# Retention of 128-position chunks recomputed in steps of 64 positions with 64x64 products, and a seven-product down projection with chained sums

## The chip, the core and the metric

The kernel runs on one core of a Trainium2 chip. Its parts, as the profile names them: PE (TensorE, matrix products; PEld is its loading of the stationary operand, which overlaps the products), DVE (VectorE), ACT (ScalarE), POOL (GpSimd), SP (SyncE, which here issues DMA). Products write to PSUM, which DVE and ACT empty. The metric is the device time of one execution in microseconds (us), and lower is better.

## What is computed

Batch 8, 8 heads, 576 positions, head size 64. For each head `h` the retention is causal and decays with distance; after it, 4608 tokens of width 512 go through an up product to 2048, an activation, and a down product to 512.

```python
scores = scale * np.matmul(q, k.transpose(0, 1, 3, 2))
Dmat = np.where(rel >= 0, gamma[:, None, None] ** rel[None, :, :], 0.0)
attn = np.matmul(scores * Dmat[None], v)          # then (B*S, H*D) = x
h = x @ w_in
g = h * np.clip(h + 3.0, 0.0, 6.0) / 6.0
out = g @ w_out
```

Retention need not form all 576x576 scores. With keys scaled by `gamma**(-position)` and queries by `gamma**position` inside a chunk, a chunk's output is a masked product inside the chunk (scores, then scores times values) plus the query times a 64x64 state per head that sums keys times values of all earlier positions.

## The kernel before

**Blocks.** The first 64 positions of all eight batches form block 0, handled by functions whose names end in `heads`. The other 512 positions of each batch are blocks 1 to 8, each of four chunks of 128 positions; chunk `c` belongs to block `c // 4`, and chunks 4 to 35 pass through the functions below. The output of a block's retention is the tile `xT`, which the up product of the same block reads.

**Up and down.** `up_unit` is a sixteenth of a block's up product: eight products of 512 columns into one PSUM bank `ph` (L163), then on ACT a Relu into `u` (L389), then on DVE the activation into `g` (L391). The bank is free again when L391 is done. The down product of blocks 0 and 1 is plain (`down_plain`, tile `pd`). From block 2 on, `down_strassen` uses seven half-size products instead of eight (112 steps, each a pair of matmuls of 256 columns, tile `pm`). It needs sums of quarters of `g` (five a half block, DVE, L407), sums of weight quarters made once (five pairs, `ws`, DVE), and sums of the results (ACT copies, adds on POOL and DVE).

**Retention of a chunk.** `casts` (k on ACT, q and v on POOL, with the decay), `transposes` (on PE for chunks before 13, by DMA on SP after), `scores` (L210: eight matmuls, two 64-row halves of the array at a time, 128 columns; two banks `pa`; two masked copies on DVE, L213), `state` (L245: eight matmuls of 64 columns into `pu`, an add on DVE L250, a product with the decay on POOL L251), `past` (the state to fp16 in a block-diagonal tile `sbd`, two ACT casts L237), `inner` (L264 with `product` at L163: scores times values and state times query into one bank `po`, eight matmuls each, 128 columns; one ACT copy to `xT`, L268).

**Array shapes.** The profile gives a matmul's shape as rows*columns of the array that it uses. Most of this kernel uses 128*64: `product` splits an output of 128 partitions into two halves, which run side by side. `scores` uses 64*128, and `by_key` of block 0 uses 128*32.

**Order.** Instructions stand on each engine in the order in which the code issues them (`manual_schedule`). For blocks 0 to 2 the strings given to `go` set it: a letter is a step (`c` cast, `t` transpose, `s` state, `z` past, `a` scores, `i` inner, `+` a pending DVE sum, `D` down steps, `L`, `R`, `U` up units). From block 2 on, the loop at the end runs sixteen times a block: one up unit of the next block, seven down steps of this one, then the retention steps that the table `STEADY` (for block 2 `FIRST_STEADY`) holds under that number, for chunks of the block after next:

```python
for _ in range(lead):
    next(down, None)
if kb + 1 < NB:
    up_unit(kb + 1, u)
...
for _ in range(per - lead):
    next(down, None)
do((w, i if w == "+" else c + i) for w, i in table.get(u, []))
```

**PSUM.** Of eight banks, six rotate in the pool `pp` (`ph`, `pa`, `pu`, `po` and the transposes, in the order in which they are asked for), and two in `st` (down products). A tile in `pp` takes the bank of the tile that was asked for six places earlier, and its first write waits until that one has been read.

The functions with the profile's line numbers:

Of the kernel before, what the change touches and what calls it, by code (L numbers as in the profile page):

```python
# [12 lines left out]
FP32 = mybir.dt.float32  # L13
# [8 lines left out]
def kernel(  # L22
# [54 lines left out]
    mask = const.tile([P, P], FP16)  # L77
    query = const.tile([P, P], FP32)
# [8 lines left out]
    sbd = [const.tile([P, NP, 2, D], FP16, name=f"sbd{i}") for i in range(2)]  # L87
# [46 lines left out]
    def others():  # L134
# [4 lines left out]
        for h in range(H):  # L139
            lo = (h % 2) * D  # L140
            nc.gpsimd.memset(gpow[lo:lo + D, h // 2:h // 2 + 1], float(gamma[h] ** P))
        for i in range(2):
            nc.gpsimd.memset(sbd[i], 0.0)

    def mask_of_chunk():
        nc.gpsimd.memset(mask, 1.0)
        nc.gpsimd.affine_select(out=mask, in_=mask, compare_op=ALU.is_ge,
                                fill=0.0, base=0, pattern=[[1, P]], channel_multiplier=-1)

# [5 lines left out]
    ws = {n: const.tile([P, JH, HM], FP16, name=f"ws{n}") for n in (1, 3, 4, 6, 7)}  # L155

    hmask = ws[4].rearrange("p j n -> p (j n)")[:, 0:H * P].rearrange("p (h q) -> p h q", h=H)
# [20 lines left out]
    def casts(c):  # L178
        fk, fq, fv = st[c]["f"]
        dd = dec[:, NJ, :].unsqueeze(2).to_broadcast([P, 2 * H, D])  # L180
        k16 = work.tile([P, H, D], FP16, tag="k16", bufs=4, name=f"k16_{c}")
        q16 = work.tile([P, H, D], FP16, tag="q16", name=f"q16_{c}")
        v16 = work.tile([P, H, D], FP16, tag="v16", bufs=NV16, name=f"v16_{c}")
        nc.scalar.copy(k16, fk)  # L184
        nc.gpsimd.tensor_tensor(q16, fq, dd[:, 0:H, :], ALU.mult)  # L185
# [3 lines left out]
    def transposes(c, on_pe):  # L189
        for nm in ("k", "q"):  # L190
            src = st[c][nm + "16"].rearrange("p h d -> p (h d)")
            dst = work.tile([P, NP, P], FP16, tag=f"{nm}T", bufs=4, name=f"{nm}T_{c}")
# [10 lines left out]
    def scores(c):  # L203
        kT, qT = st[c]["kT"], st[c]["qT"]
        a16 = work.tile([P, 2, NP, P], FP16, tag="a16", name=f"a16_{c}")
        pa = [psum.tile([P, NP, P], FP32, tag="pp", name=f"pa{h2}_{c}") for h2 in range(2)]
        for i in range(NP):
            for h2 in range(2):
                r = slice(h2 * D, h2 * D + D)
                nc.tensor.matmul(pa[h2][:, i, :], kT[r, i, :], qT[r, i, :], start=True, stop=True)  # L210
        m = mask.unsqueeze(1).to_broadcast([P, NP, P])
        for h2 in range(2):
            nc.vector.tensor_tensor(a16[:, h2], pa[h2], m, ALU.mult)  # L213
        st[c]["a16"] = a16
# [510 lines left out]
```

## Time and profile before

| what | value |
|---|---|
| median of 3 runs | 301.76 us (300.6 to 302.05) |
| the profiled execution | 300.82 us |
| its span on the core | 299.1 us |
| mean granted clock of PE | 0.994 |
| PE busy | 289.9 us (97%), 4514 matmuls |
| DVE, ACT, POOL busy | 237.9, 199.9, 151.4 us |

The span is what the profile covers; 1.7 us of the execution lie around it. Busy time counts an engine as busy while any of its instructions is under way. Matmuls overlap each other: one of 512 columns is under way for about 380 ns, but the next pair starts about 215 ns after the one before, so the starts in the timeline say more than the busy time. Granted clock 1.00 means that PE ran at full speed.

### The profile page before, as it was taken

How to read it: one execution, taken by the hardware profiler on the slowest of the kernel's cores; microseconds unless marked ns; L12 is line 12 of the kernel's file. 1: busy time of each engine (PE TensorE's matmuls, PEld its weight loads, DVE VectorE, ACT ScalarE, POOL GpSimd, SP SyncE). 2: the span in 40 equal slices, each digit the busy share in tenths (PEclk: the TensorE clock that was granted, in tenths of full speed). 3: DMA queues.
4: the chain of work that ended last, by engine and by line, in shares of the span. 5: the costliest groups of instructions: out<-in, count | busy, mean ns of one | idle time of the engine just before them, and what ended most of it. 6: DMA issues, size and time to landing. Idle time of an engine off the chain costs nothing.

```text
span 299.1 us, 10655 instructions
## 1 busy us (share of the span) xinstructions
PE 289.9 (97%) x4514; PEld 222.6 (74%) x4514; DVE 237.9 (80%) x389; ACT 199.9 (67%) x374; POOL 151.4 (51%) x182
## 2 busy tenths in 40 slices
PE   6799999999999999999999999999999999999995
PEld 2478567887665678777878787878887888778894
DVE  4739576978966868899979897989798979777972
ACT  4668966999666597766776577657765765465430
POOL 7887087555844404891388338833893353014100
PEclk9989999999999999999999999999999999999999
DMA  7999999899999999999998999999975010300122
GB/s 159 168 197 215 187 214 207 187 212 207 208 163 156 316 170 225 180 186 182 263 160 147 211 196 151 152 213 195 160 144 178 20 18 2 142 2 2 72 107 106
DMA packets 136287, 47.74 MB, mean 160 GB/s; under 512 B 125744, under 2 KB 131376, under 8 KB 136240
## 3 DMA queue, kind: packets, MB, share of 16 engines
q1 hardware_dynamic: 131088, 41.56, 72.2%
q0 software_dynamic: 4720, 5.11, 10.3%
q8 instruction: 35, 0.57, 0.8%
q10 hardware_dynamic: 432, 0.39, 0.5%
q14 instruction: 12, 0.10, 0.1%
HBM read 36.70 MB, written 9.44 MB: 154 GB/s over the span
## 4 chain that ended last, share of the span: by engine, by line
PE 83%; DMA 7%; DVE 3%; ACT 2%; SPq 1%; POOL 1%; issue 1%; POOLq 0%; DVEq 0%
PE ph L163 39%; PE pm L163 29%; PE pd L163 6%; DMA qT<-q 3%; PE pa L210 2%; PE po L163 2%; PE po L264 2%; DMA fq<-in_q_dram 2%; DMA hq<-in_q_dram 2%; DMA hk<-in_k_dram 1%; DVE g L391 1%; DVE a L213 1%; PE pu L245 1%; POOL q L185 1%; ACT u L389 1%
## 5 line engine op out<-in xcount | busy, mean ns | idle before, releaser
L163 PE MATMUL ph<-xT,win 128*64 128x512 f16 (+1 forms) x1248 | 146.4, 365 | 0.3
L389 ACT ACTIVATE u<-ph,half 128x512 f32<-128x512 f32 (+1 forms) x156 | 99.9, 657 | 59.4 <-PE ph L163 58.0
L391 DVE SCALAR_TENSOR_TENSOR g<-u,ph 128x512 f16<-128x512 f32 (+1 forms) x156 | 98.4, 643 | 37.2 <-ACT u L389 36.5
L163 PEld LDWEIGHTS <-win 128*64 128x64 f16 x1248 | 81.0, 137 | 25.0 <-issue 0.4
L251 POOL TENSOR_TENSOR z<-t,gpow 128x256 f32<-128x256 f32 x24 | 18.5, 769 | 69.8 <-DVE t L250 65.9
L163 PEld LDWEIGHTS <-g 128*64 128x64 f16 x704 | 37.9, 110 | 14.5
L163 PE MATMUL pm<-ws,s 128*64 128x256 f16 x672 | 43.8, 273 | 0.0
L163 PEld LDWEIGHTS <-s 128*64 128x64 f16 x672 | 37.0, 110 | 7.1
L185 POOL TENSOR_TENSOR q<-fq,dec 128x512 f16<-128x512 f32 x32 | 37.4, 1170 | 8.0 <-DMA fq<-in_q_dram 5.9
L407 DVE TENSOR_TENSOR s<-g 128x1024 f16<-128x1024 f16 x42 | 41.3, 988 | 0.0
L213 DVE TENSOR_TENSOR a<-pa,mask 128x512 f16<-128x512 f32 x64 | 40.3, 682 | 0.5 <-PE pa L210 0.5
L186 POOL TENSOR_TENSOR v<-fv,dec 128x512 f16<-128x512 f32 x32 | 38.6, 1208 | 0.1
L163 PE MATMUL pd<-wout,g 128*64 128x512 f16 x256 | 33.9, 381 | 0.0
L163 PE MATMUL pm<-ws,g 128*64 128x256 f16 x448 | 30.6, 273 | 0.0
L163 PE MATMUL pm<-wout,sab 128*64 128x256 f16 x448 | 30.6, 273 | 0.0
L163 PEld LDWEIGHTS <-sab 128*64 128x64 f16 x448 | 24.7, 110 | 4.8
L268 ACT CAST xT<-po 128x512 f16<-128x512 f32 x32 | 18.7, 586 | 11.9 <-PE po L163 11.8
L407 DVE TENSOR_TENSOR sab<-g 128x1024 f16<-128x1024 f16 x28 | 23.4, 839 | 0.0
L184 ACT CAST k<-fk 128x512 f16<-128x512 f32 x32 | 19.8, 619 | 0.2
L237 ACT CAST sbd<-z 64x256 f16<-64x256 f32 x48 | 19.2, 400 | 0.4
L264 PE MATMUL po<-a,v 128*64 128x128 f16 x256 | 18.1, 219 | 0.1
L163 PE MATMUL po<-qT,sbd 128*64 128x128 f16 x256 | 17.9, 219 | 0.0
(106 smaller groups left out, 272.6 us busy)
## 6 DMA issues: line engine op xcount, KB each, us to landing
fk<-in_k_dram SPq DMA_DIRECT2D x32, 256.0 KB, 4.3
fq<-in_q_dram SPq DMA_DIRECT2D x32, 256.0 KB, 4.8
fv<-in_v_dram SPq DMA_DIRECT2D x32, 256.0 KB, 5.1
out_dram<-o SPq DMA_DIRECT2D x15, 512.0 KB, 4.8
wout<-in_moe_w_out_dram POOLq DMA_DIRECT2D x4, 512.0 KB, 16.0
win<-in_moe_w_in_dram POOLq DMA_DIRECT2D x3, 512.0 KB, 9.9
out_dram<-o SPq DMA_DIRECT2D x5, 256.0 KB, 5.4
hq<-in_q_dram SPq DMA_DIRECT2D x6, 128.0 KB, 5.0
```

What stands on the lines that cost most here:

```text
L163: nc.tensor.matmul(out[r], lhs[:, r], rhs, skip_group_check=True, **flags)
L184: nc.scalar.copy(k16, fk)
L185: nc.gpsimd.tensor_tensor(q16, fq, dd[:, 0:H, :], ALU.mult)
L186: nc.gpsimd.tensor_tensor(v16, fv, dd[:, H:2 * H, :], ALU.mult)
L213: nc.vector.tensor_tensor(a16[:, h2], pa[h2], m, ALU.mult)
L237: nc.scalar.copy(sbd[i0 % 2][r, :, h2, :], z[r])
L251: nc.gpsimd.tensor_tensor(z, t, decay, ALU.mult)
L264: nc.tensor.matmul(po[h2 * D:h2 * D + D, i, :], v16[:, 2 * i + h2, :], a16[:, h2, i, :], start=(i == 0), stop=False, skip_group_check=True)
L268: nc.scalar.copy(xts[kb][:, :, i0 * P:i0 * P + P], po)
L389: nc.scalar.activation(uu[:, 0:n], ph[:, 0:n], ACTF.Relu, bias=half, scale=1.0 / 6.0)
L391: nc.vector.scalar_tensor_tensor(out=g[:, hf, ths, jr, :], in0=by_half(uu), scalar=1.0, in1=by_half(ph), op0=ALU.min, op1=ALU.mult)
L407: nc.vector.tensor_tensor(*pend.popleft())
```

## The change

A chunk is handled as two steps of 64 positions. `scores` forms only the two 64x64 diagonal squares of each head (the scores between the second half's queries and the first half's keys are replaced by the state), `states` sums keys times values of each half apart, `add` makes two states a chunk (before the first half, and before the second), `past` turns both to fp16, and the output is cross terms (state times query) and inner terms (scores times values). Every matmul of these uses 64*64 of the array and 64 columns, and the lists are issued two and two for the upper and the lower 64 rows (`in_turn`). A chunk takes 64 matmuls instead of 32 (the last chunk of a block 56 instead of 24). The two row halves are kept from adding into one bank at the same time: the cross terms that go over to the other bank (`cross_over`) come first, then the states of the next chunks, then a drain of PE (`nc.tensor.drain()`), then the rest of the cross terms and the inner terms (`inner`).

From chunk 16 on, two chunks go through these functions together, and a visit in `STEADY` is `a` of the next pair, `x` and `i` of this pair with `s` of the next between them, in steps 5 and 13 of sixteen. Chunks 4 to 15 go one at a time (scores and states share a bank there). The masked copies take half the elements, the adds on DVE go from one a chunk to two, the block-diagonal tile is gone, and heads are stored in another order so that heads `i` and `i + 4` share a transposed tile.

The down product still takes seven products of the same sizes, in the order 1, 5, 2, 3, 6, half of 4, 7, the other half of 4, with four sums of `g` a half block (each made from the one before) and four pairs of weight sums instead of five of each.

The core of the diff; removed lines of the retention functions are left out, since they stand above:

```diff
-        for i in range(2):
-            nc.gpsimd.memset(sbd[i], 0.0)
...
+        nc.gpsimd.tensor_copy(mask[SUB:P, 0:SUB], mask[SUB:P, SUB:P])
...
-        k16 = work.tile([P, H, D], FP16, tag="k16", bufs=4, name=f"k16_{c}")
-        q16 = work.tile([P, H, D], FP16, tag="q16", name=f"q16_{c}")
+        k16 = work.tile([P, NP, 2, D], FP16, tag="k16", bufs=4, name=f"k16_{c}")
+        q16 = work.tile([P, NP, 2, D], FP16, tag="q16", name=f"q16_{c}")
-        nc.scalar.copy(k16, fk)
-        nc.gpsimd.tensor_tensor(q16, fq, dd[:, 0:H, :], ALU.mult)
+        by_head = lambda t: t.rearrange("p i a d -> p a i d")
+        in_rows = lambda t: t.rearrange("p (a i) d -> p a i d", a=2)
+        nc.scalar.copy(by_head(k16), in_rows(fk))
+        nc.gpsimd.tensor_tensor(by_head(q16), in_rows(fq), in_rows(dd[:, 0:H, :]), ALU.mult)
...
+            dst = work.tile([P, NP, P], FP16, tag=f"{nm}T", bufs=dict(k=4, q=6)[nm], name=f"{nm}T_{c}")
...
+    PAIRS = 16
+    group = lambda c: [c] if c < PAIRS else [c, c + 1]
+    rows = lambda x: slice(SUB * x, SUB * x + SUB)
+    gs = {}
+    def mm(*args, **flags):
+        return lambda: nc.tensor.matmul(*args, skip_group_check=True, **flags)
+    def in_turn(by_row):
+        for n in range(0, max(len(t) for t in by_row), 2):
+            for t in by_row:
+                for x in t[n:n + 2]:
+                    x()
+    def scores(c0):
+        g = group(c0)
+        n = len(g)
+        a16 = work.tile([P, 2, 2, NP, SUB], FP16, tag="a16", bufs=4, name=f"a16_{c0}")
+        pb = [psum.tile([P, 2, NP, SUB], FP32, tag="pp", name=f"pa{a}_{c0}") for a in range(2)]
+        pa = [b[:, 0:n] for b in pb]
+        todo = ([], [])
+        for x, c in enumerate(g):
+            kT, qT = st[c]["kT"], st[c]["qT"]
+            for i in range(NP):
+                for s in range(2):
+                    for a in range(2):
+                        todo[a].append(mm(pa[a][rows(s), x, i, :], kT[rows(a), i, rows(s)], qT[rows(a), i, rows(s)],
+                                          start=True, stop=True))
+        in_turn(todo)
+        gs[c0] = dict(a16=a16, pa=pa, pu=[b[:, n:2] for b in pb])
+        if n == 2:
+            masked(c0)
+    def masked(c0):
+        n, a16, pa = len(group(c0)), gs[c0]["a16"], gs[c0]["pa"]
+        m = mask[:, 0:SUB].unsqueeze(1).to_broadcast([P, n * NP, SUB])
+        for a in range(2):
+            nc.vector.tensor_tensor(a16[:, a, 0:n].rearrange("p x i q -> p (x i) q"),
+                                    pa[a].rearrange("p x i q -> p (x i) q"), m, ALU.mult)
     decay = gpow.unsqueeze(2).to_broadcast([P, NP, D])
...
+    def states(c0):
+        g = group(c0)
+        pu = gs[c0]["pu"]
+        if len(g) == 2:
+            pu = [psum.tile([P, 2, NP, D], FP32, tag="pp", name=f"pu{s}_{c0}") for s in range(2)]
+        todo = ([], [])
+        for x, c in enumerate(g):
+            k16, v16 = st[c]["k16"], st[c]["v16"]
+            sums[c] = [pu[s][:, x] for s in range(2)]
+            for i in range(NP):
+                for s in range(2 if c % NCB < NCB - 1 else 1):
+                    for a in range(2):
+                        todo[s].append(mm(pu[s][rows(a), x, i], k16[rows(s), i, a, :], v16[rows(s), i + NP * a, :],
+                                          start=True, stop=True))
+        in_turn(todo)
+        if len(g) == 1:
+            masked(c0)
+    def state_of(c):
+        if c not in zs:
+            zs[c] = work.tile([P, 2, NP, D], FP32, tag="z", bufs=2, name=f"z{c}")
+        return zs[c]
+    def add(c):
+        kb, i0 = divmod(c, NCB)
+        z = state_of(c)
+        nc.vector.tensor_tensor(z[:, 1], sums[c][0], z[:, 0] if i0 else zh[kb - 1], ALU.add)
+        if i0 < NCB - 1:
+            new = state_of(c + 1)[:, 0]
+            nc.vector.tensor_tensor(new, sums[c][1], z[:, 1], ALU.add)
+            nc.gpsimd.tensor_tensor(new, new, decay, ALU.mult)
     def past(c):
         kb, i0 = divmod(c, NCB)
...
+        z16 = work.tile([P, 2, NP, D], FP16, tag="z16", bufs=2, name=f"z16_{c}")
+        if i0:
+            nc.scalar.copy(z16, zs[c])
+        else:
+            nc.scalar.copy(z16[:, 0], zh[kb - 1])
+            nc.scalar.copy(z16[:, 1], zs[c][:, 1])
+        z16s[c] = z16
     xts = {}
...
+    def cross(c0, flip):
+        g = group(c0)
+        todo = ([], [])
+        if "po" not in gs[c0]:
+            gs[c0]["po"] = [psum.tile([P, len(g), NP, SUB], FP32, tag="pp", name=f"po{s}_{c0}") for s in range(2)]
+        for x, c in enumerate(g):
+            for i in range(NP):
+                for a in range(2):
+                    s, cc, b = a ^ flip, i // 2 + 2 * a, i % 2
+                    todo[a].append(mm(gs[c0]["po"][s][rows(b), x, cc, :], z16s[c][rows(a), s, i, :],
+                                      st[c]["qT"][rows(a), i, rows(s)],
+                                      start=bool(flip) and x == 0 and i < 2, stop=False))
+        return todo
+    def cross_over(c0):
+        in_turn(cross(c0, 1))
+    def inner(c0):
+        kb, i0 = divmod(c0, NCB)
+        g = group(c0)
+        n = len(g)
         if kb not in xts:
             xts[kb] = work.tile([P, NP, BLK], FP16, tag="xT", bufs=2, name=f"xT{kb}")
...
+        todo = cross(c0, 0)
+        a16, po = gs[c0]["a16"], gs[c0]["po"]
+        for x, c in enumerate(g):
+            for h in range(H):
+                for s in range(2):
+                    todo[s].append(mm(po[s][rows(h % 2), x, h // 2, :], st[c]["v16"][rows(s), h, :],
+                                      a16[rows(s), h // NP, x, h % NP, :], start=False, stop=True))
+        nc.tensor.drain()
+        in_turn(todo)
+        xt = xts[kb][:, :, i0 * P:i0 * P + n * P].rearrange("p n (x s q) -> p s x n q", x=n, s=2)
+        for s in range(2):
+            nc.scalar.copy(xt[:, s], po[s])
+        for c in g:
+            del st[c], z16s[c]
+        del gs[c0]
...
-            gt[kb, jq] += [sab, s1, s67]
+            s1, s2, s3, s4 = [gp.tile([P, JQ, HB], FP16, tag=f"s{n}", bufs=b, name=f"s{n}{kb}_{jq}")
+                              for n, b in ((1, 2), (2, 2), (3, 2), (4, 2))]
+            pend.extend([(s1, g[:, 0, 1], g[:, 1, 1], ALU.add), (s2, s1, g[:, 0, 0], ALU.subtract),
+                     (s4, g[:, 1, 0], s2, ALU.subtract), (s3, g[:, 0, 0], g[:, 0, 1], ALU.subtract)])
+            gt[kb, jq] += [s1, s2, s3, s4]
...
-        prods = {1: (A(2), W(1)), 2: (A(1, 1), B11), 3: (A(0, 0, 0), W(3)), 4: (A(0, 1, 1), W(4)),
-                 5: (A(1, 0), B22), 6: (A(3, 0), W(6)), 7: (A(3, 1), W(7))}
+        lo, hi = slice(0, HM), slice(HM, DM)
+        prods = {1: (A(0, 0, 0), half_of(0, lo)), 2: (A(0, 1, 0), half_of(1, lo)), 3: (A(4), half_of(1, hi)),
+                 4: (A(0, 1, 1), W(4)), 5: (A(1), W(1)), 6: (A(2), W(2)), 7: (A(3), W(3))}
...
-        b3, by_m3 = bank(3)
-        yield from one(3, by_m3)
-        nc.scalar.copy(s3, b3)
-        b4, by_m4 = bank(4)
-        yield from one(4, by_m4)
-        nc.scalar.copy(s4, b4)
-        side.tensor_tensor(s3, s3, s4, ALU.add)
-        yield from one(5, by_m3, True)
-        nc.scalar.copy(c12, b3)
...
+        ba, by_a = bank(1)
+        yield from one(1, by_a)
+        nc.scalar.copy(p1, ba)
+        bb, by_b = bank(5)
+        yield from one(5, by_b)
+        nc.scalar.copy(p5, bb)
...
+        yield from one(2, by_a, True)
+        nc.scalar.copy(c11, ba)
...
+        yield from one(3, by_b, True)
+        nc.scalar.copy(c12, bb)
+        bc, by_c = bank(6)
+        yield from one(6, by_c)
+        nc.scalar.copy(u2, bc)
+        add(pool, u2, u2, p1)
+        add(pool, c12, c12, u2)
+        store(kb, 0, o1)
+        bd, by_d = bank(4)
+        yield from one(4, by_d, ms=(0,))
+        yield from one(7, by_c, True)
+        add(dve, u3, bc, p1)
+        add(pool, c22, p5, u3)
+        yield from one(4, by_d, ms=(1,))
+        add(dve, c21, bd, u3)
         store(kb, 1, o2)
...
-        of = {3: (b12, b22, ALU.subtract), 4: (b21, b11, ALU.subtract), 1: (b11, b22, ALU.add),
-              6: (b11, b12, ALU.add), 7: (b21, b22, ALU.add)}
+        of = {1: (b12, b11), 2: (b22, ws[1]), 3: (b22, b12), 4: (b21, ws[2])}
-                x, y, op = of[n]
-                pend.append((ws[n][:, j, :], x[:, j, :], y[:, j, :], op))
+                x, y = of[n]
+                pend.append((ws[n][:, j, :], x[:, j, :], y[:, j, :], ALU.subtract))
...
-    STEADY = {0: [("z", 0), ("s", 0), ("+", 1)], 1: [("a", 0), ("a", 1)], 2: [("z", 1), ("+", 1)],
-              3: [("i", 0), ("s", 1), ("c", 3)], 4: [("+", 1)], 5: [("z", 2)],
-              6: [("i", 1), ("s", 2), ("c", 4), ("+", 1)], 8: [("a", 2), ("a", 3), ("z", 3)],
-              9: [("+", 1)], 10: [("i", 2), ("+", 1), ("c", 5)], 11: [("+", 1)], 12: [("+", 1)],
-              13: [("i", 3), ("+", 1), ("c", 6)], 14: [("+", 1)], 15: []}
+    STEADY = {0: [("u", 1), ("+", 1)], 1: [("z", 1)], 2: [("+", 1)], 4: [("c", 4), ("+", 1)],
+              5: [("a", 2), ("x", 0), ("s", 2), ("i", 0), ("u", 2)], 6: [("c", 5), ("u", 3)],
+              7: [("z", 2), ("+", 1)], 8: [("z", 3)], 9: [("+", 1)], 11: [("+", 1)],
+              12: [("+", 1), ("c", 6)], 13: [("a", 4), ("x", 2), ("s", 4), ("i", 2), ("u", 4)],
+              14: [("c", 7), ("z", 4)], 15: [("+", 1)]}
...
-        weight_sums(4, 7)
-        weight_sums(6, 3, 1)
+        weight_sums(3)
+        weight_sums(1, 2, 4)
-        go("k0 D4 k1 D4 +1 k2 D4 +1 k3 D6 h0 D2 c4 +1 h1 D3 z4 h2 D3 +1 h3 D3 c5 D4 t4 D5 s4 a4 D5 t5 i4 "
-           "z5 c6 D4 s5 a5 +1 D7 i5 D2 t6 L2 c7 s6 a6 L3 z6 D3 t7 L1 i6 L3 a7 z7 L3 c8 D2 i7 D3 t8 R3 c9 R3 "
-           "s8 a8 z8 R2 t9 R2 c10 i8 R2 U1 s9 a9 z9 c11 U3 i9",
+        go("k0 D4 k1 D4 +1 k2 D4 +1 k3 D6 h0 D2 c4 h1 D3 h2 D3 h3 D3 c5 D4 t4 D5 a4 s4 u4 D5 t5 z4 c6 D4 "
+           "a5 x4 s5 i4 u5 +1 z5 D7 x5 D2 i5 D2 t6 L2 c7 a6 s6 u6 z6 L3 D1 t7 L3 D2 a7 x6 s7 i6 u7 z7 L3 c8 x7 D2 i7 L1 D3 "
+           "t8 R3 c9 R3 a8 s8 u8 z8 R2 t9 R3 c10 R1 a9 x8 s9 i8 u9 z9 U1 c11 t10 U3",
...
```

## The prediction

> **What bounds the kernel now.** I read the page first (busy time, then the chain that ended last), then the busy time by stretch, then PE's instructions in order of time through one block.
>
> ```profile
> PE 289.9 (97%) x4514; PEld 222.6 (74%) x4514; DVE 237.9 (80%) x389; ACT 199.9 (67%) x374; POOL 151.4 (51%) x182
> PE 83%; DMA 7%; DVE 3%; ACT 2%; SPq 1%; POOL 1%; issue 1%; POOLq 0%; DVEq 0%
> ```
>
> ```profile
> 44.00:118.50 74.50, 73.58 (x1156) 53.67 (x1156) 57.97 (x105) 57.98 (x118) 37.34 (x40) 1.00 1.07 205
> 118.50:267.00 148.50, 148.50 (x2350) 118.68 (x2346) 130.44 (x195) 98.71 (x178) 80.24 (x68) 1.00 0.81 148
> ```
>
> The second fence is the stretches (length, then busy time of PE, PEld, DVE, ACT, POOL). From 44 to 118.5 us, where chunks go one at a time, PE lacks 0.9 us; from there to 267 it lacks nothing. DVE is at 88% and limits nothing. So the time is what PE's starts take, and I price PE's starts.
>
> ```profile
> 210.54 0.22 PE L264 MATMUL po<-a,v 128*64 128x128 f16 x2
> ...
> 210.99 0.29 PE L245 MATMUL pu<-v,k 128*64 128x64 f16 x8
> 211.11 1.06 PE L163 MATMUL ph<-xT,win 128*64 128x512 f16 x8
> ...
> 213.63 0.93 PE L163 MATMUL pm<-wout,sab 128*64 128x256 f16 x14
> 214.49 0.62 PE L210 MATMUL pa<-qT,kT 64*128 64x128 f16 x16
> 215.04 1.08 PE L163 MATMUL ph<-xT,win 128*64 128x512 f16 x8
> 215.96 0.27 PE L163 MATMUL pm<-wout,sab 128*64 128x256 f16 x2
> ```
>
> Columns are start, time under way, what. An up unit takes 0.87 us to the next start (218.80 to 219.67) and its seven down steps 0.76 (219.67 to 220.43): 1.63 a unit, 26.08 for sixteen. A block takes 29.70 (first `pu` at 199.32, the next block's at 229.02), which leaves 3.62 us for the retention of four chunks. The fence shows its parts: `inner` 0.45 (210.54 to 210.99, eight pairs at 0.055), a state 0.12, and scores of two chunks. Those use another array shape: 0.10 us pass before them (213.63 + 0.76 = 214.39 to 214.49), their eight pairs need 0.44 of the 0.55 to the next start, so 0.11 passes after them, and the next up unit takes 0.92 instead of 0.87. Going into another shape and out again costs 0.26 us.
>
> **Round of four.** All retention products become 64x64 with 64 columns. The nearest row is `pu` (64 columns, pairs): eight take 0.29 with a mean of 0.196, so pairs start (0.29 - 0.196) / 3 = 0.031 us apart. If four quadrants run together, a round of four also takes 0.031: four 128*32 tiles of `hpk` do run together (16 of 128 columns from 32.01 to 32.35, less 0.12 for the change of shape, is 0.055 a round), and so do the two row halves of `pa`. The other bound is two at a time, 0.062. I take 0.031, as both splits are seen to work alone.
>
> The Trainium skill, "TensorE: Matmul & The Clock Gate", section on the 56 ns gap, says that start to start never falls below about 25 ns however few the columns. Those 16 `hpk` matmuls started 14 ns apart on average, in different tiles, so I don't apply it between tiles; its mechanism is the last rival below.
>
> **Pairs of chunks (16 to 35).** A visit is a (8 rounds, 0.25), x (4, 0.125), s (8, 0.25), drain, i (12, 0.375): 1.0 us. To it come a change of shape, a drain and a wait.
>
> Shape: 0.26, taken as for scores.
>
> Drain: no row of PE has one. Below: 0, if the array is refilled without a gap. Above: 0.30, a matmul's whole 0.196 and the 0.10 of a shape change. I take 0.22: the last products must land (0.196 less a round) and a standalone instruction in PE's queue takes 0.051 (the semaphore waits at L210).
>
> PSUM: a visit asks for six banks (two `pa`, two `po`, two `pu`) of the six in the pool, so the second `pu` gets the bank of the up unit just before the visit and waits for its `g`. The chain of such a unit, undisturbed:
>
> ```profile
> 196.06 1.03 PE L163 MATMUL ph<-xT,win 128*64 128x512 f16 x8
> ...
> 197.13 0.69 ACT L389 ACTIVATE u<-ph,half 128x512 f32<-128x512 f32 x1 [0.80 <-PE ph L163]
> ...
> 197.85 0.69 DVE L391 SCALAR_TENSOR_TENSOR g<-u,ph 128x512 f16<-128x512 f32 x1
> ```
>
> `g` ends 2.48 us after the unit's start. PE gets to that `pu` at 1.63 + 0.10 + 0.375 = 2.10. It waits 0.38, with everything behind it in PE's queue. Before step 5 ACT also has the copy of product 5 (0.58) and the k cast (0.62) ahead of `u`: the previous `u` ends 0.13 into the unit, the copies end at 1.33, `u` at 2.02, `g` at 2.74, a wait of 0.64. Mean 0.5. Bounds: 0.38, and 1.0 if a DVE sum of 0.99 falls badly.
>
> The next up unit needs the bank of the first `pa`, which DVE masks (0.68) right after that `g`: done at 3.2 or 3.4, while the visit ends at 1.63 + 1.98 = 3.6, so it hides behind the wait. The sum for product 7 ("+" of step 12) may hold PE inside unit 13, but it ends at about 1.9, ahead of the `g` that PE waits for anyway.
>
> A visit: 1.0 + 0.26 + 0.22 + 0.5 = 1.98, two a block 3.96 against 3.62. Five blocks: +1.7. The first pair has a visit of its own for a and s: +0.26.
>
> **Single chunks (4 to 15).** Before: 12 x (0.45 + 0.22) + 9 states x 0.12 + 12 scores visits x 0.26 = 12.2 us. After: 12 x 16 rounds x 0.031 = 6.0; 20 visits by the strings (cross and inner of 5, 7, 11 and 15 stand apart, with down steps between) x 0.26 = 5.2; 12 drains x 0.22 = 2.6. Together 13.8, so +1.6. Bank waits are taken as 0 here: up units are few and the banks older.
>
> **Costed at nothing.** DVE loses two sums a block of about 0.93 and half of eight masks of 0.68, and gains four adds of 0.42; ACT trades eight casts of 0.40 for three of about 0.58 and two of 0.40; POOL loses one add of 1.27 a block. None is the bound, so nothing is gained; if PE weren't, DVE's 2.9 us a block would count. The seven products are the same 112 steps. Casts and DMA transposes on SP stay as many and land seven units (11 us) ahead of their scores, against 3.5 us for a `qT`. In the last block some adds go from DVE (0.69) to POOL (1.27), with 3.5 us of products after them; its last add and store are of the same form, so the tail from PE's last start (295.25) stays.
>
> **Sum.** 300.82 (the profiled execution: 299.1 of span and 1.7 around it) + 1.7 + 0.3 + 1.6 = 304.4. The median of the runs shown is 0.9 above that execution, so a median would be near 305. The streaming of PE does fall, by 5 us over the pairs alone (from 20 x 0.67 + 15 x 0.12 = 15.2 to 10.0), and is given back as waits for a bank, drains and changes of shape.
>
> **Rivals.**
> Emptying the array is cheap (the other side). If a drain costs 0.03 and a visit only the 0.10 on the way in, 22 drains save 4.2 and 31 visits 5.0: 295. It decides when the 0.48 a visit falls below about 0.3, since 5 of those 12.9 us bring it under 299.3; taken at 297.5. For it: the new shape's price isn't in this trace. Against: two other shapes cost the same 0.10 and 0.12.
>
> Quadrants run two at a time. Pairs: 2.0 of rounds, 0.26, 0.22 and a wait of 0.15 make 2.63 a visit, 5.26 a block, +8.2 over five; singles +6.0 more than forecast: 317. For it: loads of 64*64 tiles in both row halves are nowhere seen side by side. Against: `pa`.
>
> After a drain PE's queue is empty, and i needs 96 loads and matmuls. At 12 ns each (14 began between 92.11 and 92.28, after a wait; an upper bound) i would take 1.15; at 8 ns 0.77, +0.39 on ten visits and half of that on twelve: 311.
>
> Each matmul takes a start of its own whatever its columns, as a `po` pair's 0.055 would be two of 0.0275: 64 starts a chunk are 1.76 us in place of 0.5, +40 on 32 chunks, less 5 of bank waits, 340. Against: `pu` and `hpk` started 14 to 16 ns apart. By the 25 ns of the Trainium skill's page named above it would be 334, an estimate.
>
> **Chances.** Forecast 0.55 (its own range 301 to 308.5: drains between 0.1 and 0.3, bank waits between 0.38 and 0.7), cheap emptying 0.20, slow refill 0.12, two at a time 0.10, a start each 0.03. About 0.5% (1.5 us) is what a measurement can tell from no change. Faster by more is the first rival, 0.20; within it is the forecast's lower end, 0.12; the rest, 0.68, is slower. The range runs from 297.5 to 313: it leaves out the far end of cheap emptying (0.07), and the last two rivals (0.13).
>
> **What would show it.** In PE's order of time, a round of four `pa` each 0.031 us; a wait of 0.4 to 0.7 at the second `pu` on DVE's `g` in steps 5 and 13 (in the list of waits `pu` from that `g`, ten times, some 5 us); a gap of 0.2 between the last `pu` and the first `po` after it; 0.10 before and after each visit; a block of about 30.0 us instead of 29.70; DVE's busy time down by some 20 us. The forecast is wrong if blocks take under 29.4 (drain or shape cheaper), or over 31 (rounds of 0.06, or i slower than its rounds).

## The result, and the profile after

The changed kernel takes 313.8 us (median of four runs, 311.63 to 315.3), against 301.18 (300.52 to 302.05) for the kernel before in the same comparison: a ratio of 1.041, 95% interval 1.037 to 1.045. Slower was right; the size was not: 3.6 us were forecast, 12.6 came, and the range ended at 313.0. The profiled execution took 315.30 us with a span of 313.6, which is 14.5 more than that of the kernel before.

The page after, busy time and the chain that ended last:

```profile
PE 293.2 (94%) x5538; PEld 219.4 (70%) x5538; DVE 219.3 (70%) x383; ACT 193.3 (62%) x361; POOL 140.9 (45%) x177
PE 77%; DVE 10%; ACT 6%; issue 3%; DMA 3%; SPq 0%; ACTq 0%; DVEq 0%
```

PE had 97% of the span and now has 94%; DVE and ACT, 5% of the chain before, hold 16%. So PE waits. The stretches that the prediction showed, and the list of PE's waits:

```profile
44.00:118.50 74.50, 71.75 (x1542) 48.95 (x1540) 55.15 (x114) 52.66 (x114) 35.92 (x37) 1.00 0.95 195
118.50:267.00 148.50, 138.83 (x2760) 108.64 (x2756) 110.53 (x173) 91.12 (x160) 69.42 (x63) 0.99 0.92 146
```

```profile
PE pu L212 <- DVE g L467: 4.3, 8, 0.9
PE pa L212 <- DMA qT<-q: 3.4, 1, 3.4
```

From 118.5 to 267 us PE, which lacked nothing before, lacks 9.7 us. The two waits are 7.7 of them.

To see what the work itself takes I gave every pair or round of four matmuls its regular distance to the next one (0.2155 us for 512 columns, 0.1093 for 256, 0.0555 for 128, 0.0312 for 64). These add up to 274.1 us before and 265.3 after: streaming fell by 8.8, near the forecast (5.2 for the pairs and, by the prediction's terms, 9.1 - 6.0 = 3.1 for the single chunks). What is left of the time between PE's first and last start, gaps, went from 19.2 to 42.9.

Where they came in, by the starts of PE's products in both executions:

| up to | before | after | grown by |
|---|---|---|---|
| first up unit | 17.84 | 18.60 | 0.76 |
| unit 0 of block 1 | 50.23 | 52.02 | 1.02 |
| loop of block 2 (FIRST_STEADY) | 108.66 | 112.91 | 2.47 |
| loop of block 3 (STEADY) | 138.84 | 149.36 | 6.27 |
| loop of block 7 | 257.63 | 271.88 | 3.72 |
| PE's last start | 295.25 | 310.15 | 0.66 |
| end of the span | 299.12 | 313.60 | -0.41 |

The first row is mostly not the change: in the experiments below that start lies anywhere between 16.93 and 19.01. The second holds the first two single chunks: from chunk 4's first product to unit 0 of block 1 it is 6.82 us in the kernel before and in "down only" below, which has its retention, and 7.74 or 7.75 in the changed kernel and in all runs below with the new retention and one drain a chunk, so 0.92 of its 1.02 are the change. The third holds the other ten single chunks, the fourth the first three visits of pairs, the fifth four steady blocks (two of them, 181.20 to 242.78, take 30.79 us each instead of 29.70; the last has no new scores in step 13).

A visit of step 13, PE in order of time:

```profile
204.69 0.93 PE L162 MATMUL pm<-ws,s 128*64 128x256 f16 x14
205.55 0.45 PE L212 MATMUL pa<-qT,kT 64*64 64x64 f16 x32
205.82 0.30 PE L212 MATMUL po<-qT,z 64*64 64x64 f16 x16
205.95 0.22 PE L212 MATMUL pu<-v,k 64*64 64x64 f16 x2
207.03 0.44 PE L212 MATMUL pu<-v,k 64*64 64x64 f16 x30 [0.87 <-DVE g L467]
207.62 0.32 PE L212 MATMUL po<-qT,z 64*64 64x64 f16 x16
207.76 0.46 PE L212 MATMUL po<-a,v 64*64 64x64 f16 x32
208.14 1.08 PE L162 MATMUL ph<-xT,win 128*64 128x512 f16 x8
```

The rounds of `pa` start 0.032 us apart (the first 0.053): eight in the 0.27 from 205.55 to 205.82. 0.10 us pass before them (204.69 + 0.76 = 205.45). The first pair of `pu` starts at 205.95, the rest at 207.03: 1.08, of which 0.02 is regular. From 207.03 to the first `po` behind the drain are 0.59 us, of which 0.25 are eight rounds: about 0.3 for the drain. The whole visit, from 205.45 to 208.14, takes 2.69 us. In step 5 the same lines have the wait at `pu` at 0.39 and the visit at 1.96.

Why the `g` is late in step 13, on DVE and on POOL:

```profile
202.36 0.69 DVE L467 SCALAR_TENSOR_TENSOR g<-u,ph 128x512 f16<-128x512 f32 x1 [0.94 <-ACT u L465]
202.97 1.74 DVE L478 TENSOR_TENSOR s<-s,g 128x1024 f16<-128x1024 f16 x1
204.62 0.67 DVE L467 SCALAR_TENSOR_TENSOR g<-u,ph 128x512 f16<-128x512 f32 x1
205.22 1.16 DVE L478 TENSOR_TENSOR s<-g,s 128x1024 f16<-128x1024 f16 x1
206.31 0.67 DVE L467 SCALAR_TENSOR_TENSOR g<-u,ph 128x512 f16<-128x512 f32 x1
```

```profile
202.88 1.27 POOL L546 TENSOR_TENSOR u<-u,p 128x512 f32<-128x512 f32 x1 [6.86 <-ACT u L582]
204.23 1.60 POOL L546 TENSOR_TENSOR o<-o,u 128x512 f32<-128x512 f32 x1
```

The sums of steps 11 and 12 stand ahead of the last two `g`, and they take 1.74 and 1.16 us where others take 0.68. POOL's two adds after product 6 run beside them. The `u` of unit 13 was there at 205.59 (ACT from 204.90, 0.69), so the last `g` started 0.72 late.

And the other wait, in the visit of step 7 of FIRST_STEADY, with the granted clock behind it in a stretch:

```profile
126.32 0.32 PE L212 MATMUL pa<-qT,kT 64*64 64x64 f16 x16
130.00 0.32 PE L212 MATMUL pa<-qT,kT 64*64 64x64 f16 x16 [3.36 <-DMA qT<-q]
...
131.57 1.93 PE L162 MATMUL ph<-xT,win 128*64 128x512 f16 x8
133.28 1.49 PE L162 MATMUL pm<-wout,s 128*64 128x256 f16 x14
```

```profile
131.50:134.00 2.50, 2.50 (x28) 1.35 (x19) 0.90 (x3) 1.54 (x3) 1.42 (x2) 0.50 1.67 208
```

Chunk 18's scores start, chunk 19's wait 3.4 us for its `qT`. The column after the five engines is the clock: 0.50, and an up unit of 1.93 us instead of 1.03. Its four pairs started 0.21 later each than at full clock (0.80 in all), the first five pairs of the down steps behind it 0.10 to 0.11 each (0.56), and the end of the visit lost 0.2: some 1.5 us. The Trainium skill, "TensorE: Matmul & The Clock Gate", section "What's actually happening", has the clock fall to half after an idle window of about 3.4 us. With this wait, the trace agrees; shorter waits stand in the last section.

### The profile page after: what moved, and what is told of

It is laid out like the page before. It is cut to its first block, busy times and chain, and to the rows that moved or that the text cites. A ratio compares the mean times of both kernels' runs of the same rounds, so it can differ in the third digit from the quotient of the medians.

```text
span 313.6 us, 12656 instructions
## 1 busy us (share of the span) xinstructions
PE 293.2 (94%) x5538; PEld 219.4 (70%) x5538; DVE 219.3 (70%) x383; ACT 193.3 (62%) x361; POOL 140.9 (45%) x177
## 4 chain that ended last, share of the span: by engine, by line
PE 77%; DVE 10%; ACT 6%; issue 3%; DMA 3%; SPq 0%; ACTq 0%; DVEq 0%
PE ph L162 36%; PE pm L162 22%; PE pd L162 9%; DVE g L467 5%; ACT u L465 4%; PE po L212 4%; DVE s L478 4%; DMA hq<-in_q_dram 2%; PE pa L212 1%; PE pu L212 1%; DMA qT<-q 1%; PE hptq L389 1%; ACT k L185 1%; ACT hqT L393 1%; PE hpo L434 1%
## 5 line engine op out<-in xcount | busy, mean ns | idle before, releaser
L162 PEld LDWEIGHTS <-s 128*64 128x64 f16 x896 | 49.9, 111 | 10.9 <-issue 1.1
L293 POOL TENSOR_TENSOR z<-z,gpow 128x256 f32<-128x256 f32 x24 | 16.7, 698 | 74.0 <-DVE z L292 60.2
L342 ACT CAST xT<-po 128x256 f16<-128x256 f32 (+1 forms) x44 | 18.5, 473 | 33.2 <-PE po L212 33.2
L162 PE MATMUL pm<-wout,g 128*64 128x256 f16 x448 | 31.8, 273 | 0.0
L244 DVE TENSOR_TENSOR a<-pa,mask 128x256 f16<-128x256 f32 (+1 forms) x44 | 21.8, 536 | 5.9 <-PE pa L212 5.8
L478 DVE TENSOR_TENSOR s<-g 128x1024 f16<-128x1024 f16 x28 | 21.7, 773 | 0.0
L299 ACT CAST z<-z 128x512 f16<-128x512 f32 x24 | 14.8, 617 | 3.9 <-DVE z L289 3.5
L478 DVE TENSOR_TENSOR s<-s,g 128x1024 f16<-128x1024 f16 x14 | 17.2, 1226 | 0.0
L162 PE MATMUL pm<-wout,s 128*64 128x256 f16 x224 | 17.0, 279 | 0.0
L162 PE MATMUL pm<-ws,g 128*64 128x256 f16 x224 | 16.4, 273 | 0.0
```

The source lines that it names most:

```text
L162: nc.tensor.matmul(out[r], lhs[:, r], rhs, skip_group_check=True, **flags)
L244: nc.vector.tensor_tensor(a16[:, a, 0:n].rearrange("p x i q -> p (x i) q"), pa[a].rearrange("p x i q -> p (x i) q"), m, ALU.mult)
L293: nc.gpsimd.tensor_tensor(new, new, decay, ALU.mult)
L342: nc.scalar.copy(xt[:, s], po[s])
L478: nc.vector.tensor_tensor(*pend.popleft())
```

## The experiments

My theory after the two traces was that the gaps around the pairs' visits made the loss: a bank not yet free, an emptied array, a late transpose. The rivals were the new down product with its chained sums, and drains of another price. In the table, "block" is the mean of the loops of blocks 4 and 5, "step 5" and "step 13" are the waits at the second `pu` beyond its regular distance in block 5's visits, "qT" is the largest wait of the two later visits of FIRST_STEADY, all in us from the one profiled execution of each.

| kernel | median | ratio to before, 95% | block | step 5 | step 13 | qT |
|---|---|---|---|---|---|---|
| changed | 313.8 | 1.041 (1.037-1.045) | 30.79 | 0.39 | 1.06 | 3.4 |
| down only | 302.26 | 1.001 (0.999-1.004) | 29.74 | - | - | 0 |
| retention only | 316.75 | 1.049 (1.043-1.055) | 31.41 | 1.06 | 0.89 | 1.9 |
| later visit | 313.69 | 1.040 (1.034-1.046) | 30.79 | 0.39 | 1.06 | 1.9 |
| filled | 312.58 | 1.034 (1.031-1.038) | 30.41 | 0 | 0.96 | 3.8 |
| sum later | 313.44 | 1.039 (1.032-1.046) | 30.79 | 0.39 | 1.06 | 1.9 |
| sum later, filled | 312.19 | 1.036 (1.032-1.041) | 30.38 | 0 | 0.95 | 1.9 |
| early casts | 314.52 | 1.041 (1.034-1.048) | 30.79 | 0.39 | 1.06 | 1.0 |
| second drain | 315.76 | 1.049 (1.043-1.054) | 31.40 | 0.39 | 1.05 | 1.6 |
| sums apart | 312.73 | 1.040 (1.032-1.048) | 30.11 | 0.39 | 0.39 | 3.2 |
| sums apart, filled | 310.22 | 1.028 (1.021-1.034) | 29.66 | 0 | 0 | 1.3 |
| two on PE | 310.5 | 1.028 (1.024-1.032) | 30.78 | 0.39 | 1.06 | 0 |
| all three | 308.94 | 1.023 (1.018-1.027) | 30.14 | 0 | 0 | 0 |
| POOL adds later | 312.02 | 1.034 (1.030-1.038) | 30.11 | 0.39 | 0.39 | 2.1 |

**Each half of the change alone.** First the new down product with the retention of before; its eight sums a block stand in eight of the steps where ten stood.

> Retention of the kernel before, the new down product alone (order 1, 5, 2, 3, 6, 4, 7, four chained sums a half block, four pairs of weight sums). Theory (the time went into PE's new gaps around the retention): PE streams the same products, so 300.5 to 302.5 us, a ratio to the kernel before of 1.000 within 0.005. Rival (the chained sums, 1.2 to 1.7 us on DVE where one took 1.0, hold up g and so PE): at least 4 us slower, 305 or more, with PE waiting for g in the up units.

302.26 us, ratio 1.001: the theory's side. The down product with its chained sums costs nothing as long as PE doesn't wait for DVE.

> The new retention alone, with the down product, the sums and the weight sums of the kernel before; four buffer counts are one lower so that it fits the memory (a16 3, v16 5, qT 5). Theory: most of the loss stays, only the longer wait in step 5 (1.06 us against 0.64 forecast, five times) can go, some 2 us: 311 us, ratio 1.033 (1.025 to 1.04). Rival (the chained sums made the loss): 307 or less, ratio under 1.02.

316.75, more than with both halves, so the rival falls, and so does my expectation that some of the wait would go. The old sums are ten a block and not eight, and they stand ahead of the banks' `g` too: waits of 1.06 and 0.89 at `pu`, blocks of 31.41. At 217.66 one of them, issued just ahead of the `g` for step 5, takes 1.81 us beside a POOL add. The new down product, free by itself, spares the new retention about 0.6 us a block.

**The late transpose.** The first attempt was to ask for chunk 19's scores two steps later, and to cast it a step earlier:

```diff
-    FIRST_STEADY = {0: [("+", 1), ("c", 2)], 1: [("a", 0), ("s", 0), ("u", 0)], 2: [("z", 0), ("u", 1), ("c", 3)],
+    FIRST_STEADY = {0: [("+", 1), ("c", 2)], 1: [("c", 3), ("a", 0), ("s", 0), ("u", 0)], 2: [("z", 0), ("u", 1)],
...
-                    7: [("a", 2), ("x", 0), ("s", 2), ("i", 0), ("u", 2)], 8: [("c", 5), ("z", 2), ("u", 3)],
-                    9: [("z", 3)], 10: [("+", 1)], 11: [("+", 1)], 12: [("+", 1), ("c", 6)],
+                    8: [("c", 5)], 9: [("a", 2), ("x", 0), ("s", 2), ("i", 0), ("u", 2)],
+                    10: [("z", 2), ("u", 3), ("+", 1)], 11: [("z", 3), ("+", 1)], 12: [("+", 1), ("c", 6)],
```

> The changed kernel, with FIRST_STEADY alone altered: chunk 19 is cast one step earlier and the visit of step 7 stands in step 9. Theory (late DMA transposes of chunk 19 cost 3.4 us of wait and about 1.5 us of products at half clock after it): 309 us, 4 to 5 us less than the changed kernel, and the wait for qT gone. Rival (the wait covers another one, for the states of chunks 17 and 18 or for a bank, which would then show): 312 to 314.

313.69: not told from the changed kernel. The wait left step 9's visit (0.39 there, for a bank), and the visit of step 13 waited 1.9 us for chunk 21's `qT`. So it isn't one late cast but a rate. SP's queue in the changed kernel:

```profile
113.64 0.57 SPq L172 DMA_DIRECT2D fk<-in_k_dram  x1
114.26 0.57 SPq L172 DMA_DIRECT2D fq<-in_q_dram  x1
114.88 1.64 SPq L172 DMA_DIRECT2D fv<-in_v_dram  x1
116.61 2.38 SPq L483 DMA_DIRECT2D out_dram<-o  x1
119.11 1.40 SPq L200 DMA_TRANSPOSE kT<-k  x1
120.61 1.22 SPq L200 DMA_TRANSPOSE qT<-q  x1
```

It has no pause: the `kT` of chunks 16 to 21 are issued at 104.4, 110.7, 119.1, 125.3, 130.9 and 136.7, 6.5 us apart, with loads and stores between. The same stretch of time for the engines (the last two columns are the DMA engines' busy share, above 1 since packets in flight overlap, and GB/s), first of the kernel before, then of the changed one:

```profile
113.00:149.00 36.00, 36.00 (x582) 28.38 (x580) 32.31 (x52) 24.76 (x47) 20.48 (x18) 1.00 1.17 210
149.00:270.00 121.00, 121.00 (x1897) 96.97 (x1892) 105.35 (x154) 79.59 (x143) 63.23 (x54) 1.00 0.70 130
```

```profile
113.00:149.00 36.00, 31.44 (x660) 24.23 (x658) 25.60 (x40) 21.11 (x39) 14.95 (x15) 0.95 1.12 182
149.00:270.00 121.00, 115.79 (x2318) 90.81 (x2316) 91.09 (x143) 74.84 (x130) 54.85 (x49) 1.00 0.85 138
```

The DMA engines were as busy in the kernel before (1.17, and 0.70 once that stretch is over), and nothing waited; its scores of chunks 18 and 19 came at 128.4 and 130.5, one at a time, while the pair asks for both at 126.3. Then the same casts earlier:

```diff
-    FIRST_STEADY = {0: [("+", 1), ("c", 2)], 1: [("a", 0), ("s", 0), ("u", 0)], 2: [("z", 0), ("u", 1), ("c", 3)],
+    FIRST_STEADY = {0: [("+", 1), ("c", 3)], 1: [("a", 0), ("s", 0), ("u", 0)], 2: [("z", 0), ("u", 1), ("c", 4)],
...
-        go("U1 D3 U1 D2 U1 U1 D2 a14 x13 s14 i13 u14 z14 o1 U1 D2 c16 U1 D2 U1 D2 U1 D2 +1 U1 a15 x14 s15 i14 u15 z15 "
-           "D2 U1 D2 c17 +1 U1 D2 +1 U1 D2 x15 +1 U1 i15 +1 U1 D2 U1 U1",
+        go("c16 U1 D3 U1 D2 U1 U1 D2 a14 x13 s14 i13 u14 z14 o1 U1 D2 c17 U1 D2 U1 D2 U1 D2 +1 U1 a15 x14 s15 i14 u15 z15 "
+           "D2 U1 D2 c18 +1 U1 D2 +1 U1 D2 x15 +1 U1 i15 +1 U1 D2 U1 U1",
```

> The changed kernel, with the casts of chunks 16 to 23, and so their DMA transposes and the loads behind them, one place earlier each (chunk 16 at the start of the third string, 17 where 16 was, and so on). Theory (SP issues transposes, loads and stores of chunks 16 to 21 without a pause from 104.4 to 141 us, 6.1 us a chunk, and that queue is what makes qT of chunk 19 late): SP starts this some 6 us earlier, the visit of step 7 doesn't wait, 4.5 to 5 us less, 309. Rival (DMA itself or the loads are late, and the transposes only follow them; or another wait stands behind): 312 or more, with qT or kT still waited for.

314.52, the rival's side: SP's transposes started only 2.7 us earlier (101.7), and both later visits still waited for `qT`, 1.0 and 0.7 us. Moving work to an earlier place on this path made the waits shorter and not the time. Taking work from it did both:

```diff
-            if c >= PE_T:
+            if c >= PE_T and c not in (18, 19):
...
-                    3: [("+", 1), ("z", 1)], 4: [("+", 1)], 5: [("c", 4)], 6: [("+", 1)],
+                    3: [("+", 1), ("z", 1)], 4: [("t", 2), ("+", 1)], 5: [("t", 3), ("c", 4)], 6: [("+", 1)],
```

> The changed kernel, with chunks 18 and 19 transposed on PE (in steps 4 and 5 of FIRST_STEADY) and not by DMA. Theory (from 18 to about 145 us the DMA engines have no time left, and the visits of FIRST_STEADY, which ask for two chunks at once and earlier than before, meet that): four DMA transposes less, some 6 us of SP and DMA time ahead of chunks 20 and 21, so the waits for qT (3.4 us) and the half clock after them (1.3) go, PE pays 1.0 for the transposes; 3.5 us less, 310, and less scatter from run to run. Rival (PE waits there for casts or banks anyway): 313 or more, with waits of pa or of the transposes for POOL or ACT.

310.5, as expected (310), no wait for `qT` in the list, and the visit runs through:

```profile
126.24 0.45 PE L212 MATMUL pa<-qT,kT 64*64 64x64 f16 x32
126.51 0.30 PE L212 MATMUL po<-qT,z 64*64 64x64 f16 x16
```

The scatter fell too: four runs between 310.19 and 310.77, against 311.63 to 315.3 for the changed kernel. Which of the two, SP's queue or the DMA engines, sets the rate isn't separated: the edit relieves both. The DMA share from 113 to 149 us is 1.08 here, against 1.12 with the wait, so the share marks a busy stretch and doesn't tell what limits it.

**The wait for a bank.** Products of the same block moved ahead of the visits, so that PE comes later to `pu`:

```diff
+                more = {1: -2, 2: -2, 3: -2, 4: -2, 5: 8, 10: -1, 11: -2, 12: -2, 13: 5}.get(u, 0) if table is STEADY else 0
...
-                for _ in range(per - lead):
+                for _ in range(per - lead + more):
```

> The changed kernel, with down steps moved in STEADY alone: unit 5 takes 15 of them instead of 7 and unit 13 takes 12, both ahead of their visit, and units 1 to 4 and 10 to 12 give them up; the total and the order of the products stay. Theory (PE waits at the second pu because it is there before DVE has freed the bank): 4 to 4.5 us less, near 309.5, and the waits of pu for g gone from the list. Rival (DVE and ACT can't keep up with up units that stand 0.22 us closer together, so the wait moves to ph in units 2 to 5): 313 or more.

312.58. The wait of step 5 went; that of step 13 stayed at 0.96 although PE had 0.55 us more to do, since PE asks for unit 13 earlier and DVE isn't done earlier. I read this as step 5's wait, the long one, and moved the wrong sum:

```diff
-    STEADY = {0: [("u", 1), ("+", 1)], 1: [("z", 1)], 2: [("+", 1)], 4: [("c", 4), ("+", 1)],
-              5: [("a", 2), ("x", 0), ("s", 2), ("i", 0), ("u", 2)], 6: [("c", 5), ("u", 3)],
+    STEADY = {0: [("u", 1), ("+", 1)], 1: [("z", 1)], 2: [("+", 1)], 4: [("c", 4)],
+              5: [("a", 2), ("x", 0), ("s", 2), ("i", 0), ("u", 2)], 6: [("c", 5), ("+", 1), ("u", 3)],
```

> The changed kernel, with one DVE sum a block moved: the sum of step 4 in STEADY goes to step 6, behind the visit. Theory (two sums of 1.74 and 1.16 us just ahead of the g that frees the bank hold up DVE; ACT has that unit's u ready at 205.59, so g could end at 206.27 and not 206.98): the wait at pu in step 5 falls from 1.06 to about 0.36 us, four times, so 2.8 us less than the changed kernel, 311. Rival (the sum only moves the wait on, to ph of the next units or to the masks): 313.5 or more.

> As the run before, and besides 6 down steps more ahead of the visit of step 5 (from units 1 to 4) and 5 more ahead of that of step 13 (from units 10 to 12). Theory: with DVE freed the extra products now cover what is left of both waits, so pu waits for g no more in STEADY and the time is 5.5 to 6 us below the changed kernel, 308. Rival (DVE is the bound of steps 0 to 5 whatever stands in which step, as the filled kernel before suggests): no more than the run before, 311.

The second has the fill as well, with 6 steps at unit 5 instead of 8. Both waits stayed as they were in the first (0.39 and 1.06), and the second did what the fill alone had done. Counting units from a block's start put it right: 1.06 belongs to step 13. So the sums of steps 11 and 12 were moved:

```diff
-              7: [("z", 2), ("+", 1)], 8: [("z", 3)], 9: [("+", 1)], 11: [("+", 1)],
-              12: [("+", 1), ("c", 6)], 13: [("a", 4), ("x", 2), ("s", 4), ("i", 2), ("u", 4)],
-              14: [("c", 7), ("z", 4)], 15: [("+", 1)]}
+              7: [("z", 2), ("+", 1)], 8: [("z", 3)], 9: [("+", 1)], 10: [("+", 1)],
+              12: [("c", 6)], 13: [("a", 4), ("x", 2), ("s", 4), ("i", 2), ("u", 4)],
+              14: [("c", 7), ("z", 4), ("+", 1)], 15: [("+", 1)]}
...
```

> The changed kernel, with the DVE sums of steps 11 and 12 moved to 10 and 14 in STEADY (in FIRST_STEADY to 9 and 14). The run with the sum of step 4 moved left both waits as they were, 0.39 and 1.06: the long wait stands in step 13, not in step 5 as I had it. Theory (the chained sums of 1.74 and 1.16 us that are issued in steps 11 and 12 hold up the g that frees the bank for step 13): the wait of step 13 falls from 1.06 to 0.39 as in step 5, four times, 2.7 us less in STEADY, and blocks of 30.1 instead of 30.8. Rival (the masks, adds or casts of step 13 itself, or ACT, set that wait): it stays at 1.06.

The wait of step 13 is 0.39, blocks take 30.11: as the theory had it. The time (312.73) doesn't tell it from the changed kernel; the wait for `qT` was 3.2 us there, and from block 3's loop to the end the profiled execution is 1.4 us shorter, not 2.7. With four steps more ahead of each visit:

```diff
+                more = {3: -2, 4: -2, 5: 4, 11: -2, 12: -2, 13: 4}.get(u, 0) if table is STEADY else 0
...
```

> As the run before, and 4 down steps (0.43 us) more ahead of the visits of steps 5 and 13, taken from units 3, 4, 11 and 12. Theory: with DVE free PE gets to the second pu just as g is done, both waits fall under 0.05, blocks of 29.4 us, below the 29.7 of the kernel before, 5.5 us less than the changed kernel from 149 us on. Rival (the wait goes on to the up units): blocks of 30 or more.

310.22 us, 3.6 less than the changed kernel and not 5.5, and no wait at `pu` is left. Blocks of 29.66 and not 29.4: without any wait at `pu` the new retention takes what the old one took (29.70). Next, whether two sums in that place are enough, or POOL's adds beside them are needed:

```diff
+        bd, by_d = bank(4)
+        yield from one(4, by_d, ms=(0,))
+        yield from one(7, by_c, True)
         add(pool, u2, u2, p1)
         add(pool, c12, c12, u2)
         store(kb, 0, o1)
-        bd, by_d = bank(4)
-        yield from one(4, by_d, ms=(0,))
-        yield from one(7, by_c, True)
```

> The changed kernel, its DVE sums in steps 11 and 12 as they are; only POOL's two adds after product 6 (and the store behind them) are issued after product 7 instead, some three units later. Theory (the sum of step 11 takes 1.74 us and not 0.68 because it runs beside a POOL add of 1.27, which begins just before it; that of step 12 takes 1.16 for the same reason): both sums take 0.68, g of unit 13 starts when its u is ready, and the wait of step 13 falls from 1.06 to 0.39, four times, 2.7 us from 149 us on. Rival (two sums in front of that g are enough, whatever POOL does): the sums stay above 1 us or the wait stays above 0.8.

DVE ahead of a visit of step 13, with the sums where they were, and PE at the second `pu`:

```profile
200.54 0.68 DVE L478 TENSOR_TENSOR s<-s,g 128x1024 f16<-128x1024 f16 x1
201.56 0.69 DVE L467 SCALAR_TENSOR_TENSOR g<-u,ph 128x512 f16<-128x512 f32 x1 [0.34 <-ACT u L465]
202.17 0.69 DVE L478 TENSOR_TENSOR s<-g,s 128x1024 f16<-128x1024 f16 x1
203.19 0.69 DVE L467 SCALAR_TENSOR_TENSOR g<-u,ph 128x512 f16<-128x512 f32 x1 [0.34 <-ACT u L465]
```

```profile
203.52 0.22 PE L212 MATMUL pu<-v,k 64*64 64x64 f16 x2
203.93 0.44 PE L212 MATMUL pu<-v,k 64*64 64x64 f16 x30 [0.19 <-DVE g L467]
```

The sums take 0.68 and 0.69, DVE is early for both `g`, and PE's wait is 0.39 again (203.52 to 203.93, less 0.02). Two sums are harmless; POOL's adds at their side made the long wait. The median is 312.02.

**The drain's price.**

```diff
-        todo = cross(c0, 0)
+        todo = ([], [])
...
+        nc.tensor.drain()
+        in_turn(cross(c0, 0))
         nc.tensor.drain()
         in_turn(todo)
```

> The changed kernel with a second drain in inner, between the cross terms and the inner terms, 22 more in all. Theory (a drain lets the last products land and starts the array afresh, 0.28 to 0.31 us beyond a round each time): 22 x 0.29 = 6.4 us more than the changed kernel, 320. Rival (the gap seen at the drain is a change of operands or the states' end, and a drain itself costs the 0.05 us of an instruction): 1.1 us more, 315.

The same visit of step 13 in that kernel:

```profile
208.93 0.32 PE L212 MATMUL po<-qT,z 64*64 64x64 f16 x16
209.40 0.45 PE L212 MATMUL po<-a,v 64*64 64x64 f16 x32
```

Between the two `po` are now 0.47 us instead of 0.14. Over the 22 drains the added gaps sum to 6.3 us (12 of 0.27, seven of 0.32, three of 0.27): the theory's price. Yet the time grew by 2.0 only, 2.8 in the profiled spans. The drains before 113 us put PE 2.4 us behind the changed kernel there, and 1.3 behind at the next block's start, since chunk 19's `qT` was waited for 1.6 us and not 3.4: what PE loses ahead of a late transpose is taken off the wait for it. Leaving the drain out wasn't tried: it stands there to keep the two row halves from adding into one bank at once.

**Together.** The sums apart with four steps of fill, and two chunks on PE:

> Sums apart, filled visits and two chunks on PE together. If the three are separate they add up: 313.8 - 5.5 - 3.5 = 305, still above the kernel before (301.2) by the drains and shape changes of the single chunks. If the DMA engines bound the whole stretch up to 149 us, the part of the fill that lies there is lost, 306 to 307.

308.94, better by 4.9 than the changed kernel, and neither 305 nor 306 to 307: the two gains of 3.6 and 3.3 don't add up in full. It is still 2.3% above the kernel before. PE has no wait at `pu` in STEADY and none for `qT`; in FIRST_STEADY, which has no fill, two waits of 0.39 at `pu` are left. The blocks of 30.14 hold a gap of 0.67 us in one up unit (187.0 to 189.3) that no run explains; without it they would be 29.8. In its profile PE is 4.3 us later than before at block 2's loop, 6.0 at block 3's, 5.9 at block 7's and 6.7 at the end: most of what remains lies ahead of the pairs, in the single chunks and the start. No run altered how the single chunks are handled, so their share is read from the gaps and not tested. No version here points below the kernel before, and none was sought further.

## Why the prediction was wrong in size

**Round of four: right.** 0.032 us against 0.031. With it fall the rivals of quadrants two at a time and of a start each; the rounds behind a drain are 0.034 apart, so the slow refill falls as well. The Trainium skill's 25 ns, weighed there, don't hold between tiles: the 32 `pa` start 8 ns apart on average. Its page "TensorE: Matmul & The Clock Gate" has another figure for that in the section "The mechanism", about 4 ns between the starts of matmuls in different tiles; the trace agrees (3 to 4 ns within a round).

**Streaming falls, and is given back: right.** 8.8 us in all, and the run with no wait at `pu` left shows blocks equal to before's.

**Shape 0.26: right.** 0.10 in, 0.11 out, 0.05 on the next products.

**Drain 0.22: too small by a third.** 0.28 to 0.31 in the pairs, 0.25 to 0.36 in the singles: at the upper one of its bounds, 0.30. The rival of a cheap emptying falls.

**PSUM wait 0.5 a visit: the step that failed in the steady blocks.** It was 0.39 in step 5, where 0.64 was forecast for ACT's copies, and 1.06 in step 13, where 0.38 was (the first was forecast too high; the second lies above the upper bound of 1.0). The sentence that failed is that the sum of step 12 "ends at about 1.9, ahead of the `g` that PE waits for anyway". It took a sum's mean of 0.93 for its duration. The page before showed the form's mean of 0.988 and not its spread, 0.68 alone and up to 1.80 beside POOL; and POOL's adds had moved with the order of the products. Of the 0.75 us that a steady block takes beyond the forecast, 0.43 are these waits and 0.14 the two drains.

**"Casts and DMA transposes land seven units (11 us) ahead of their scores": false in FIRST_STEADY.** Chunk 19's cast stands five units ahead of its visit, and its `qT` was issued at 127.1, after the scores were due at 126.4. What I priced was the latency of a `qT` (3.5 us); what was missing was the load of the path, though the stretches that I quoted carried it in the column before the last: 1.07 from 44 to 118.5 us. It cost about 3.4 + 1.5 us of the profiled execution, the largest single term of the miss, and 3.3 of the median by the run that took these transposes off the DMA path. The half clock behind the wait had no term at all.

**Single chunks +1.6: less than half of what came.** 3.4 grew there: 0.9 in chunks 4 and 5 and 2.5 in the other ten. Twelve drains at 0.30 instead of 0.22 are 0.9 of the 1.8 that lack. The rest is waits, taken as 0: sorting the gaps from chunk 4 to block 2's loop by what stands around them, I find about 2.1 us of them before and 2.9 after. No run separates the two.

**Costed at nothing, the rest: right.** The down product alone came to 1.001, and the tail even lost 0.4 us; DVE has 18.6 us less to do, as forecast (20).

In sum the span grew by 14.5 where 3.6 were forecast: single chunks 1.8 more; the visits of FIRST_STEADY 5.6 more, with 4.9 for the late `qT` and the half clock behind it; the steady blocks 2.4 more (three of them 0.75 each and one wait of 0.98 at 162.1 for a `g`, less 0.9 in block 6, whose step 13 asks for no new scores); the end 0.3 more; and the start 0.9, mostly scatter.

## What to carry to other kernels

A lower sum of starts is worth nothing on an engine that then waits: for each bank or tile that a regrouped visit asks for, follow its last reader back through the engine that frees it, with the longest duration that such an instruction has in the trace and not its mean. Before work is asked for in larger pieces, follow the queue that feeds it and read the DMA share of that stretch: here the share was above one and the queue had no pause, so transfers that were due earlier came late; issuing them earlier didn't shorten the time, and having fewer of them did. Where an edit seems to do nothing, check first that it stands in the step that the wait belongs to.

## What the runs showed of the hardware

A DVE sum of two fp16 tiles (128x1024) took 0.676 to 0.694 us in all 24 cases after 110 us in the changed kernel in which no POOL instruction ran beside it, and 1.13 on average in the 28 with one, up to 1.80. The one at 202.97 took 1.74: 1.06 until about where POOL's add ends (204.15), then its own 0.68. The POOL add behind it took 1.60 instead of 1.27. The Trainium skill, "SBUF — State Buffer", section "SBUF: two separate sides", says that DVE instructions with two SBUF inputs and POOL instructions that read SBUF share a pair of ports that the first holds for its whole instruction; the trace agrees, and the run with POOL's adds elsewhere shows what that was worth here, 0.67 us at each visit of step 13 (blocks of 30.11 instead of 30.79).

A wait much shorter than the 3.4 us that the Trainium skill gives ("TensorE: Matmul & The Clock Gate", section "What's actually happening") can bring PE's clock down: in the run with the later visit PE lacked 2.1 us at 139.7, and had a clock of 0.60 from 143.6 to 146.0; in the run with the second drain it lacked 1.8 at 128.9, and had 0.50 from 132.2 to 135.5. In the run with the sum later a wait of 2.05 at 125.6 left no product behind it at the slower distance. What decides between the two isn't settled.
